# A second matrix product as seven block products for eight, with streamed weights and a transposed result, in an attention and feed-forward kernel

## The chip, the cores and the metric

The kernel runs on one core of a Trainium2 chip. A core has a matrix engine (TensorE, PE in the profile), a vector engine (VectorE, DVE), a scalar engine (ScalarE, ACT), a general engine (GpSimd, POOL) and a queue that issues transfers (SyncE, SP). They run side by side and wait for one another by semaphores. The metric is the device time of one execution in microseconds (us), lower is better. For a program on one core, runs agree to some tenths of a per cent; all runs quoted here count as fast ones. Before the change the time was 1672.99 us (median of 3 runs, 1670.59 to 1674.83).

## The reference

```python
# q, k, v: (8, 12, 448, 64); w_in: (768, 2048); w_out: (2048, 768)
q_n, k_n = rmsnorm(q, g_q), rmsnorm(k, g_k)
scores = np.matmul(q_n, k_n.transpose(0, 1, 3, 2)) / np.sqrt(64)
attn = softmax(scores)
x = np.matmul(attn, v).transpose(0, 2, 1, 3).reshape(3584, 768)
h = x @ w_in                       # first product
g = np.maximum(h, 0.0) ** 2
out = g @ w_out                    # second product
```

The weights arrive as 64-bit floats and are turned into 32-bit floats inside the kernel ("rounding" below), chunk by chunk, with integer and float instructions on VectorE, ScalarE and GpSimd.

## The kernel before

The work goes in four spans of two batches. A "unit" is a pair of heads of one batch; there are 12 units in a span. The first attention has nothing beside it but the rounding of `w_in`. Then come, three times, a first product of a span and an attention of the next span with the second product laid between its matmuls; then the last first product and the last second product, alone.

The first product already uses seven block products for eight: the operands are cut into 2 x 2 blocks, sums of blocks are multiplied, and sums of the seven results give the four result blocks. The weight blocks and their sums are made once, written to device memory (`w1s`) and streamed back for each span. The second product is a plain one, from weights that stay in SBUF, the working memory on the chip:

```python
def second_product(work, span):
    for t in range(0, 2 * S, P):                       # 7 blocks of 128 tokens
        osb = work.tile([P, DM], F32, tag="osb", name="osb")
        for half in range(2):
            cols = slice(half * HALF, (half + 1) * HALF)
            po = ps_m.tile([P, HALF], F32, tag="m", name="po")
            for f in chunks:                           # 16
                nc.tensor.matmul(po, gT[:, f, t:t + P], w2[:, f, cols], ...)
                ...                                    # after the last: copy to osb, osb to memory
                yield                                  # after each matmul
```

The end of a unit of attention. `pavs` is the sum of values and `tots` the sum of the exponents; each has one buffer in PSUM (the memory that the matmuls write to), which the next unit needs:

```python
def finish(work, i):
    rec = work.tile([P, S], F32, tag="rec", name="rec", bufs=1)
    nc.vector.reciprocal(rec, tots.pop(i))
    nc.vector.tensor_tensor(xT[...], pavs.pop(i)..., rec..., ALU.mult)
    ...
```

In the first attention the exponents are summed by TensorE (`pe_sums`, a product with ones). In the later ones GpSimd and VectorE add the four blocks of exponents, and TensorE has only one product with ones, to save TensorE time.

## Time and profile before

| stage | us | TensorE busy, us | GpSimd busy, us |
|---|---|---|---|
| attention of span 0, rounding of `w_in` | 192.2 | 145.0 | 144.1 |
| first product of span 0, rounding of `w_out` | 150.5 | 136.2 | 69.8 |
| attention of span 1 beside second product of span 0 | 257.9 | 249.2 | 115.7 |
| first product of a later span | 127 to 129 | all | 29 to 34 |
| last second product, to the end | 150.4 | 144.5 | 1.0 |

The table is read from the windows view, whose rows give the busy time of each engine in a stretch. Where TensorE is busy for the whole of a stretch, only less TensorE work makes it shorter. Where it is not, one must ask what it waits for. The prediction shows the lines; one more piece is VectorE at the end of a unit of the first attention whose end no rounding disturbs (timeline view; start, duration, engine, line, operation, output and inputs):

```profile
103.22 2.96 DVE L585 RECIPROCAL rec<-tot 128x448 f32<-128x448 f32 x1 [6.91 <-PE tot L577]
106.09 1.16 DVE L517 TENSOR_REDUCE rstd<-qkn 112x16 f32<-112x1024 f32 x1
107.17 0.94 DVE L586 TENSOR_TENSOR xT<-pav,rec 128x448 f32<-128x448 f32 x1
```

The next unit's first values matmul starts at 108.20 us, after the multiply. Between the reciprocal and the multiply stands a reduction of another unit's normalisation.

### The profile page before, as it was taken

To read this page: it belongs to the slowest core of one execution; us is meant where nothing else is said; L and a number is where in the kernel's file an instruction comes from. 1 tells how busy PE (TensorE), PEld (TensorE's weight loads), DVE (VectorE), ACT (ScalarE), POOL (GpSimd) and SP (SyncE) were. 2 spreads that over 40 slices of the span, in tenths; PEclk is the share of its full clock that TensorE was granted. 3 is DMA by queue.
4 is the path that set the end of the run, shared out by engine and by line. 5 is a ranking of instruction groups with operands and counts; after the bars stand their busy time and mean duration, and the time that the engine had idled before them with its cause. 6 is when DMAs were issued, how large, how long until landed. Compare 5 with 4: busy or idle time off the path is not lost.

```text
span 1667.2 us, 14210 instructions
## 1 busy us (share of the span) xinstructions
PE 1556.5 (93%) x5392; PEld 771.7 (46%) x5392; DVE 550.1 (33%) x548; ACT 452.5 (27%) x621; POOL 659.1 (40%) x482
## 2 busy tenths in 40 slices
PE   5768788899999999999999999999999999999998
PEld 2223244444444455554444445554444445555554
DVE  4676589323333332122333331122333341111000
ACT  4566346232222301122222211123222221110000
POOL 5787645345455412235444421224554521221000
PEclk9989999999999999999999999999999999999999
DMA  3655445321111113331111102331111102330000
GB/s 118 204 188 185 176 164 194 101 84 43 43 43 43 43 39 86 89 102 46 43 43 44 43 20 82 89 85 48 43 43 54 41 20 61 86 89 21 19 19 21
DMA packets 93393, 125.29 MB, mean 75 GB/s; under 512 B 7300, under 2 KB 87684, under 8 KB 93316
## 3 DMA queue, kind: packets, MB, share of 16 engines
q1 hardware_dynamic: 93316, 124.29, 24.3%
q8 instruction: 45, 0.74, 0.2%
q14 instruction: 32, 0.26, 0.0%
HBM read 102.24 MB, written 22.02 MB: 75 GB/s over the span
## 4 chain that ended last, share of the span: by engine, by line
PE 84%; DVE 4%; POOL 3%; issue 3%; ACT 3%; DMA 2%; SPq 0%; DVEq 0%; POOLq 0%; ACTq 0%
PE po L690 36%; PE sc L545 8%; PE pav L566 8%; PE pd L636 8%; PE pc L636 8%; PE pa L636 7%; PE pb L636 4%; PE tot L577 3%; PE pt L534 2%; ACT qkT L536 1%; DMA w1s<-gT 1%; POOL gT L450 1%; DVE gT L400 1%; POOL rstd L519 1%; DVE gT L401 1%
## 5 line engine op out<-in xcount | busy, mean ns | idle before, releaser
L690 PE MATMUL po<-w,gT 128*128 128x384 f32 x1792 | 597.4, 490 | 0.0
L690 PEld LDWEIGHTS po<-w,gT 128*128 128x128 f32 x1792 | 334.5, 190 | 269.1 <-issue 51.0
L641 POOL TENSOR_TENSOR gT<-gT 128x448 f32<-128x448 f32 x128 | 123.6, 968 | 384.8 <-ACT gT L640 384.8
L585 DVE RECIPROCAL rec<-tot 128x448 f32<-128x448 f32 x48 | 141.9, 2956 | 279.8 <-PE tot L577 279.8
L548 ACT ACTIVATE pr<-sc 112x896 f32<-112x896 f32 x192 | 166.1, 914 | 215.5 <-PE sc L545 215.4
L566 PE MATMUL pav<-pr,vt 112*64 112x448 f32 x768 | 177.2, 572 | 38.5 <-issue 38.5
L545 PE MATMUL sc<-qkT 64*112 64x448 f32 x768 | 172.2, 568 | 0.7 <-ACT qkT L536 0.7
L518 POOL TENSOR_SCALAR rstd<-rstd 112x16 f32<-112x16 f32 x48 | 37.6, 784 | 321.4 <-DVE rstd L517 320.5
L636 PE MATMUL pa<-xT,sw 128*128 128x448 f32 x384 | 156.8, 545 | 3.1 <-DVE rec L585 3.1
L519 POOL TENSOR_TENSOR rstd<-rstd,mhalf 112x16 f32<-112x16 f32 x48 | 142.5, 2968 | 4.0
L640 ACT ACTIVATE gT<-gT 128x448 f32<-128x448 f32 x96 | 55.2, 575 | 302.8 <-DVE gT L665 183.2
L536 ACT ACTIVATE qkT<-pt,gains 128x448 f32<-128x448 f32 x96 | 59.4, 632 | 276.2 <-PE pt L534 276.2
L517 DVE TENSOR_REDUCE rstd<-qkn 112x16 f32<-112x1024 f32 x48 | 58.2, 1212 | 186.3 <-ACT qkn L514 186.0
L566 PEld LDWEIGHTS pav<-pr,vt 112*64 112x64 f32 x768 | 49.8, 141 | 149.7 <-issue 147.0
L636 PEld LDWEIGHTS pa<-xT,sw 128*128 128x128 f32 x384 | 74.0, 193 | 76.0 <-issue 71.2
L521 POOL TENSOR_TENSOR qkn<-qk,rstd 112x512 f32<-112x512 f32 x96 | 100.8, 1071 | 3.8
L534 PE MATMUL pt<-ident,qkn 112*128 112x112 f32 x384 | 55.1, 271 | 45.6 <-ACT qkT L536 24.2
L545 PEld LDWEIGHTS sc<-qkT 64*112 64x112 f32 x768 | 61.7, 175 | 76.7 <-issue 64.7
L636 PE MATMUL pd<-xT,sw 128*128 128x448 f32 x192 | 80.1, 554 | 9.7 <-DVE z L656 9.7
L556 POOL TENSOR_TENSOR acc<-acc,pr 112x896 f32<-112x896 f32 x36 | 75.0, 2084 | 33.7 <-DVE acc L556 33.7
L554 POOL TENSOR_TENSOR acc<-pr 112x896 f32<-112x896 f32 x36 | 74.9, 2081 | 28.7 <-ACT pr L548 28.7
L696 ACT COPY osb<-po 128x384 f32<-128x384 f32 x28 | 13.4, 479 | 264.1 <-PE po L690 264.1
(61 smaller groups left out, 1294.7 us busy)
## 6 DMA issues: line engine op xcount, KB each, us to landing
sw<-w1s SPq DMA_DIRECT2D x224, 192.0 KB, 2.4
gT<-in_moe_w_in_dram SPq DMA_DIRECT2D x16, 768.0 KB, 6.6
gT<-in_moe_w_out_dram SPq DMA_DIRECT2D x16, 768.0 KB, 4.3
qk<-in_q_dram SPq DMA_DIRECT2D x48, 224.0 KB, 3.4
qk<-in_k_dram SPq DMA_DIRECT2D x48, 224.0 KB, 3.6
vt<-in_v_dram SPq DMA_DIRECT2D x48, 224.0 KB, 2.8
w1s<-gT SPq DMA_DIRECT2D x8, 1344.0 KB, 7.5
out_dram<-osb SPq DMA_DIRECT2D x28, 384.0 KB, 2.7
```

What stands on the lines that cost most here:

```text
L519: nc.gpsimd.tensor_tensor(rflat, rflat, mhalf, ALU.pow)
L521: nc.gpsimd.tensor_tensor(qkn[:, s].rearrange("p j h d -> p h j d"), qk[:, s].rearrange("p h (j d) -> p h j d", d=D), rstd[:, s].rearrange ...
L534: nc.tensor.transpose(pt[:, j * SP:(j + 1) * SP], qkn[:, s, j].rearrange("p h d -> p (h d)"), ident[:SP, :SP])
L536: nc.scalar.activation(qkT[:, s], pt, AF.Copy, scale=gains[:, s:s + 1])
L545: nc.tensor.matmul(sc[:, h, 0:S], qkT[rows, 1, c * SP:(c + 1) * SP], qkT[rows, 0, :], start=True, stop=True)
L548: nc.scalar.activation(pr, sc[:, :, 0:S], AF.Exp)
L556: (nc.vector if c == 2 else nc.gpsimd).tensor_tensor(accs[i], accs[i], pr, ALU.add)
L566: nc.tensor.matmul(pavs[i][h * D:(h + 1) * D, :], vs[i][:, h, c, :], pr[:, h, :], start=(c == 0), stop=(c == NJ - 1))
L585: nc.vector.reciprocal(rec, tots.pop(i))
L636: nc.tensor.matmul(ps, stream[n][:, c], rhs[:, c], start=first and c == 0, stop=c == HC - 1, skip_group_check=not first)
L641: nc.gpsimd.tensor_tensor(g, g, g, ALU.mult)
L690: nc.tensor.matmul(po, gT[:, f, t:t + P], w2[:, f, cols], start=(f == chunks[0]), stop=(f == chunks[-1]))
```

## The change

The second product, too, is to take seven block products for eight. That needs sums of the blocks of `w_out` (made once, written to memory as `w2s`, streamed back), sums of the blocks of its input (`combine`), and more room, so `w2` no longer stays in SBUF. The result now comes out transposed; TensorE transposes it back on the way out. Twice as many chunks now go through the costlier rounding with block sums, in 35 steps. They are spread: 10 in the first attention (19 before), 14 in the first product of span 0, and 11 in the first ten half units of the second attention (a unit is issued in two halves), which for that reason run without the second product. Units are normalised two ahead, not one, and the tokens stay in another order, so that the multiply in `finish` writes in order.

```diff
-    w2 = consts.tile([P, NFC, DM], F32, name="w2")
 ...
+    gC = consts.tile([P, 3, HF, S], F32, name="gC")
 ...
+    w2s = dram.tile([HC, 7, HF // 4, P, 4 * P], F32, name="w2s")
 ...
-        qkn = loads.tile([SP, 2, NJ, 2, D], F32, tag="qkn", name="qkn", bufs=1)
+        qkn = loads.tile([SP, 2, NJ, 2, D], F32, tag="qkn", name="qkn", bufs=2)
 ...
-        nc.vector.tensor_tensor(xT[:, t, hp, :].rearrange("d (p j) -> d j p", j=NJ),
-                                pavs.pop(i).rearrange("d (j p) -> d j p", j=NJ),
-                                rec.rearrange("d (j p) -> d j p", j=NJ), ALU.mult)
+        nc.vector.tensor_tensor(xT[:, t, hp], pavs.pop(i), rec, ALU.mult)
 ...
-            if i + 1 < end:
-                norm(i + 1)
+            if i + 2 < end:
+                norm(i + 2)
 ...
+    def combine(f):
 ...
+        sub(gC[:, 0, f], g12, g11, ALU.subtract)
+        sub(gC[:, 1, f], g22, gC[:, 0, f], ALU.subtract)
+        sub(gC[:, 2, f], g21, gC[:, 1, f], ALU.subtract)
+        sub(g12, g22, g12, ALU.subtract)
 ...
+        for m in range(HC):                        # in second_product
+            for i in uses2:                        # the seven block products
+                ps = ps_m.tile([P, S], F32, tag="m", name="ps")
+                for c in range(HF):
+                    load_blocks(n + 5)
+                    nc.tensor.matmul(ps, stream[n][:, c % 4], rhs_of[i][:, c], start=c == 0, stop=c == HF - 1)
 ...
+        def deliver(ct, col, t):
+            pt = ps_m.tile([P, 512], F32, tag="m", name="po")
+            for j in range(NJ):
+                nc.tensor.transpose(pt[0:SP, j * P:(j + 1) * P], ct[:, j * SP:(j + 1) * SP], ident)
+            osb = work.tile([SP, NJ, P], F32, tag="osb", name="osb")
+            nc.scalar.copy(osb.rearrange("p j n -> p (j n)"), pt[0:SP])
 ...
+    EARLY, ALONE = 10, 10
+    LATE = 2 * NFC + 3 - 11
 ...
+                    if u < alone:
+                        weights(LATE + 11 * (u + 1) // alone)
+                    elif u == alone and span == 0:
+                        for f in range(HF):
+                            combine(f)
```

## The prediction

> **What bounds the kernel now.** I read the page's busy line first, then a table by windows cut at the stage borders, then the chain that ended last, then the timeline of TensorE in the first stage, then the groups of GpSimd work.
>
> ```profile
> PE 1556.5 (93%) x5392; PEld 771.7 (46%) x5392; DVE 550.1 (33%) x548; ACT 452.5 (27%) x621; POOL 659.1 (40%) x482
> ...
> PE   5768788899999999999999999999999999999998
> ...
> POOL 5787645345455412235444421224554521221000
> ```
>
> TensorE is the bound from the ninth slice on. Before that it is not, and there GpSimd and VectorE are the fullest. The windows say how much. Columns: stretch, its length, then busy us and instruction count of PE, PEld, DVE, ACT, POOL, then granted clock, DMA share, GB/s.
>
> ```profile
> 18.35:208.00 189.65, 145.01 (x664) 56.89 (x664) 121.73 (x108) 107.78 (x132) 144.09 (x112) 0.90 0.53 172
> 210.50:300.00 89.50, 75.61 (x187) 36.12 (x188) 77.32 (x85) 48.83 (x65) 47.28 (x31) 0.96 0.54 183
> 300.00:361.00 61.00, 60.55 (x160) 30.51 (x162) 14.81 (x23) 14.37 (x24) 22.54 (x21) 0.95 0.29 81
> 361.00:619.00 258.00, 249.31 (x969) 123.10 (x966) 83.82 (x67) 68.02 (x89) 115.66 (x69) 1.00 0.14 42
> 619.00:747.00 128.00, 127.55 (x346) 64.51 (x346) 25.70 (x41) 24.25 (x43) 34.09 (x35) 1.00 0.32 90
> ...
> 1516.80:1667.20 150.40, 144.52 (x449) 84.81 (x447) 4.52 (x8) 3.93 (x8) 1.00 (x2) 0.99 0.05 19
> ```
>
> These are, in order: attention of the first pair of batches with the rounding of all of w1; the first part of the first product with the rounding of w2; its rest; attention of the next batches laid between the second product; a first product without weight work; and the last second product, alone. The two middle stages come three times. The first two rows hold about 45 and 14 us in which TensorE is idle, and a clock below 1; everything after is TensorE work end to end.
>
> ```profile
> 618.87 2.25 PE pa L636 x6
> 621.12 2.25 PE pb L636 x6
> 623.37 2.25 PE pc L636 x6
> ...
> 1516.84 144.49 PE po L690 x448
> ```
>
> The chain gives the true pace (busy means overlap): six instructions, three matmuls of 448 columns, in 2.255 us (step from 621.12 to 623.37 and on to 625.63), so 0.752 us a matmul; 448 instructions, 224 matmuls of 384 columns, in 144.49 us, so 0.645 us. Both are 1.68 ns a column: there is no fixed cost per matmul to win.
>
> **What the Trainium skill says.** "TensorE: Matmul & The Clock Gate", section "Part 1: The HAM clock gate", says that an idle stretch of about 3.4 us or more drops the clock to half, and takes as long to end. The trace agrees: after the 5.18 us pause below, four instructions span 1.76 us that span 0.97 us after a pause of 2.43 us.
>
> ```profile
> 108.20 0.97 PE L566 MATMUL pav<-pr,vt 112*64 112x448 f32 x4 [2.43 <-issue]
> ...
> 116.21 0.98 PE L534 MATMUL pt<-ident,qkn 112*128 112x112 f32 x8
> 117.13 1.76 PE L545 MATMUL sc<-qkT 64*112 64x448 f32 x8
> ...
> 124.07 1.76 PE L566 MATMUL pav<-pr,vt 112*64 112x448 f32 x4 [5.18 <-issue]
> ```
>
> "SBUF — State Buffer", section "SBUF: two separate sides", says that GpSimd and some VectorE operations lock each other out of a shared port pair. The trace fits: the same rounding multiply of 128x384 on GpSimd ran four in 4.07 us at 99.5 us and four in 5.22 us at 116.8 us, and its mean is 1323 ns. "PSUM — Partial Sum Buffer", section "Summary: rules for kernel authors", says that transfer to memory must go by way of an engine and SBUF; so the transposed result costs a PSUM copy as well as the transpose.
>
> **The change, part by part.**
>
> *Second product.* Removed: 224 matmuls of 384 columns a span, 144.5 us. Added: 3 x 7 x 8 = 168 of 448 columns, 168 x 0.752 = 126.3 us. That is 18.2 us a span. Also added: 12 output tiles of four transposes. Eight transposes of the same kind take 117.13 - 116.21 = 0.92 us above, so four take about 0.5; 12 x 0.5 = 6 us. Each is followed by a product whose PSUM buffer is being emptied (two buffers, and the transpose has taken the other): a VectorE add of this form takes 0.62 us, with some 0.3 us of pipeline and signalling, less the 0.5 us of transposes, so about 0.4 us of wait, 12 x 0.4 = 5 us. Net 126.3 + 11 = 137.5 us for 144.5: a gain of **7 us a span, 28 us in four**. This is all on TensorE, in stages that it bounds. The four extra subtractions per f (0.62 us each) and the seven adds per block row are on VectorE, which has 84 busy of 258 us there, so free. The streamed weights, 42 blocks of 256 KB in some 250 us, are well under the 90 GB/s that the first product already streams.
>
> *First stage.* 19 rounding steps become 10, and the normalisation is taken one unit earlier. The 12 units now take 189.65 us, 15.8 each. A unit that no rounding disturbs takes 13.1 us (transposes at 103.10 and 116.21), of which TensorE has 10.7 and waits 2.43 for the division at the end of a unit. In that wait VectorE does the reciprocal of 2.96 us, a reduction of the next normalisation of 1.16 us and the multiply of 0.94 us. With the reduction earlier and the multiply writing in order (0.62, as for other operations of its size) the unit should come to 11.8 us. So 12 x 11.8 = 142, plus 4 us of start, plus half of the 25 us by which the disturbed units exceed 13.1, less a little: 10 us. Sum 156 for 189.65: a gain of **34 us**.
>
> *First product of the first span.* It took 150.5 us against the undisturbed 128: 22 us lost to 16 chunks of w2. Now 14 steps lie in it, wider apart but heavier: each has two multiplies (2 x 1.32 us) and half of four additions of 1.0 us, 4.7 us of GpSimd for 2.0. I take 20 us of loss: a gain of 2 us.
>
> *The new stretch.* Ten of the 24 half units of the second attention now run with eleven rounding steps and no second product, because w2 is not ready before. TensorE has 5 x 8.5 = 42 us of work there (258 - 144.5 is 113 us for 12 units, 9.4 with waits). GpSimd has 5 normalisations (0.8 + 2.97 + 2 x 1.07 = 5.9 us) = 30, ten sums of 2.08 = 21, and ten chunks x 4.7 = 47: together 97 us, or about 87 where no lock stretches them. VectorE has 72 us. So **GpSimd becomes the bound** here. Then the last weights must be written to memory (the same write of w1 takes 7.5 us to land) and read back (2.4 us) before the first matmul. I take 105 us from the end of the first product to the first second-product matmul. After it: 137.5 us of second product and 6.5 units at 9.4, 61 us. Sum 303.5 for 258: a loss of **45 us**.
>
> Sum: -34 - 2 + 45 - 7 - 7 (two more joint stages) - 6 (the last, which ends with a copy and a transfer behind the transposes) = -11 us, from 1673 to some 1660.
>
> **The rivals.**
> First, the new stretch hides well: GpSimd is in step with a TensorE that paces each unit at some 12 us, and the stretch lasts 65 to 70 us. Against it: the 97 us of summed durations. If so the time is about 1625, faster.
> Second, the rounding moved into the first product stalls it: a load of w1 waits on GpSimd at the head of the one DMA queue, the weight stream waits behind it and behind 1344 KB writes of 7.5 us, while the stream is now only four blocks, 9 us, ahead. The stretch would need 56 x 192 + 14 x 768 + 7 x 1344 KB, some 31 MB, in 130 us: 240 GB/s, above the 212 GB/s of the busiest 50 us seen (100 to 150 us). For it: that arithmetic; against: no TensorE wait on such a load shows in the list of waits. It would add 20 to 30 us: 1685.
> Third, the deliveries cost more than 0.9 us each, for example by TensorE waiting for both PSUM buffers whenever attention's own transposes want one. At 1.5 us each the whole gain of the second product is gone: 1690.
> Fourth, the first stage stays disturbed, with stalls over 3.4 us that also halve the clock: 15 us back, 1675.
>
> **Range and chances.** The two large terms, -34 and +45, come from the same engine's queue and have errors of some 10 and 15 us; the second product's 28 us has an error of 8, the first product's of 10. Together about 22 us, so eight times in ten 1660 - 35 to 1660 + 35. The border of faster by 2% is 1639.5, about one such error away; the author's choice of ten and ten suggests a stretch fitted to the work, which speaks for the first rival. Chances: faster 0.2, same 0.76, slower 0.04.
>
> **What would show it.** Right: the last second product at 137 us from its first to its last matmul, with 0.7 to 1.1 us between blocks at each delivery; attention of the first stage ending near 174 us; GpSimd 85% busy or more and TensorE about 40% busy in the stretch after the first product, 95 to 115 us long; later joint stages of 250 us. Wrong: a last product above 144 us would break the first step; a stretch under 80 us breaks the claim that GpSimd bounds it, and then the kernel is faster by over 2%; a first product over 165 us would mean that its stream waited.

## The result, and the profile after

The changed kernel takes 1680.94 us (median of 4 runs, 1677.65 to 1683.29), the kernel before 1673.91 in the same rounds. The ratio is 1.0042, with a 95% interval of 1.0017 to 1.0067: a little slower, and within 2%. Ratios here and below are the mean time of one kernel's fast runs over that of the other's of the same rounds, so they are not quite the ratios of the medians.

First the busy line and the slices of the changed kernel:

```profile
PE 1524.6 (91%) x5136; PEld 711.4 (42%) x5136; DVE 643.9 (38%) x732; ACT 472.4 (28%) x653; POOL 705.2 (42%) x530
...
PE   4887899964599999999999999999999999999998
...
POOL 6665367799742430224555450224555420221000
```

TensorE is busy for 32 us less in sum, as a saving of block products should have it, but the span grew from 1667.2 to 1679.0 us. There is a new hole in the TensorE row, the ninth to eleventh slices, where GpSimd is full. The windows at the stage borders say how wide it is (columns as in the prediction):

```profile
18.28:196.80 178.52, 142.49 (x664) 55.83 (x664) 98.94 (x84) 90.11 (x112) 113.06 (x91) 0.90 0.36 111
196.80:333.10 136.30, 132.65 (x345) 66.36 (x345) 72.79 (x96) 57.11 (x82) 90.28 (x82) 0.97 0.70 231
333.10:452.47 119.37, 60.28 (x230) 22.39 (x229) 76.80 (x69) 53.36 (x65) 112.84 (x72) 0.71 0.49 154
452.47:655.18 202.71, 194.79 (x677) 90.80 (x678) 72.07 (x82) 42.95 (x58) 64.12 (x38) 0.99 0.29 84
...
783.00:1032.10 249.10, 238.53 (x905) 106.68 (x906) 91.50 (x85) 72.68 (x96) 115.54 (x69) 1.00 0.29 84
...
1535.30:1679.00 143.70, 134.41 (x385) 68.49 (x383) 15.72 (x26) 9.09 (x16) 0.96 (x2) 0.99 0.32 90
```

The third row is the new stretch of attention with rounding and no second product; the fourth, "the joint rest" below, is what is left of that attention, with the second product. In the stretch TensorE works for half of the time, at a mean clock of 0.71 (60.3 us, for 42 predicted at full clock), and GpSimd is busy for 112.8 of 119.4 us. Set side by side:

| stage | before, us | after, us | difference |
|---|---|---|---|
| first attention | 192.2 | 178.5 | -13.7 |
| first product of span 0 | 150.5 | 136.3 | -14.2 |
| second attention and second product of span 0 | 257.9 | 119.4 + 202.7 = 322.1 | +64.2 |
| the same of spans 1 and 2 | 257.7 and 256.0 | 249.1 and 248.0 | -8.6 and -8.0 |
| last second product, to the end | 150.4 | 143.7 | -6.7 |

The three later first products differ by half a us or less each. The rows sum to +13.0, with these to +11.8, the difference of the spans.

The gain of the second product is there. In its last pass, alone on TensorE (timeline view, three products and two deliveries):

```profile
1619.00 6.28 PE L715 MATMUL ps<-gT,sw 128*128 128x448 f32 x16 [0.28 <-DVE ct L729]
1625.12 0.60 PE L705 MATMUL po<-ident,ct 128*112 128x128 f32 x4
1625.99 6.28 PE L715 MATMUL ps<-gT,sw 128*128 128x448 f32 x16 [0.28 <-DVE ct L729]
1632.11 0.60 PE L705 MATMUL po<-ident,ct 128*112 128x128 f32 x4
1632.90 6.28 PE L715 MATMUL ps<-gT,sw 128*128 128x448 f32 x16 [0.19 <-ACT p L721]
```

A delivery costs 1625.99 - 1625.12 = 0.87 us, transposes and the wait for the buffer together. Eight matmuls take 6.1 us.

In the new stretch, this is what TensorE waits for (timeline, the last three units):

```profile
403.14 1.76 PE L578 MATMUL tot<-acc,ones 112*64 112x448 f32 x4 [13.43 <-POOL acc L557]
...
427.50 1.76 PE L578 MATMUL tot<-acc,ones 112*64 112x448 f32 x4 [12.35 <-POOL acc L557]
...
450.55 1.76 PE L578 MATMUL tot<-acc,ones 112*64 112x448 f32 x4 [11.03 <-POOL acc L557]
```

It waits for the softmax sums, which stand in GpSimd's queue behind rounding work. And GpSimd's own instructions are slow there. At one place in it, GpSimd and VectorE side by side (timeline):

```profile
411.52 6.83 POOL L457 TENSOR_TENSOR gC<-gC 128x384 f32<-128x384 f32 x1
...
412.31 0.55 DVE L435 TENSOR_SCALAR gC<-gC 128x768 uint32<-128x768 uint32 x1
412.79 0.61 DVE L632 TENSOR_TENSOR gC<-gT 128x448 f32<-128x448 f32 x1
...
417.52 1.64 DVE L443 SCALAR_TENSOR_TENSOR gC<-gC 128x768 f32<-128x768 uint32 x1
```

The same addition took 0.99 us in the first stage (at 113.61 us). Here its record spans a run of ten VectorE instructions without a gap. In the whole stretch the 20 block sums took 36.4 us on GpSimd (groups of its instructions; count, busy us, mean ns of one, idle time before):

```profile
L457 POOL TENSOR_TENSOR gC<-gC 128x384 f32<-128x384 f32 x5 | 12.2, 2444 | 0.4
...
L456 POOL TENSOR_TENSOR gC<-gC 128x384 f32<-128x384 f32 x5 | 10.2, 2032 | 0.3
L459 POOL TENSOR_TENSOR gC<-gC 128x384 f32<-128x384 f32 x5 | 7.4, 1479 | 0.4
L458 POOL TENSOR_TENSOR gC<-gC 128x384 f32<-128x384 f32 x5 | 6.6, 1326 | 0.2
```

### The profile page after: what moved, and what is told of

Same layout as the page of the kernel before. It is cut to its first block, busy times and chain, and to the rows that moved or that the text cites. A ratio compares the mean times of both kernels' runs of the same rounds, so it can differ in the third digit from the quotient of the medians.

```text
span 1679.0 us, 14449 instructions
## 1 busy us (share of the span) xinstructions
PE 1524.6 (91%) x5136; PEld 711.4 (42%) x5136; DVE 643.9 (38%) x732; ACT 472.4 (28%) x653; POOL 705.2 (42%) x530
## 4 chain that ended last, share of the span: by engine, by line
PE 78%; POOL 8%; issue 4%; DMA 3%; DVE 3%; ACT 3%; SPq 1%; POOLq 0%; DVEq 0%; ACTq 0%
PE ps L715 31%; PE pav L567 8%; PE sc L546 8%; PE pa L646 7%; PE pd L646 7%; PE pc L646 7%; PE tot L578 4%; PE pb L646 4%; POOL gC L451 2%; PE pt L535 2%; POOL acc L557 1%; DMA gC<-in_moe_w_out_dram 1%; ACT qkT L537 1%; POOL gC L457 1%; DMA w2s<-gC 1%
## 5 line engine op out<-in xcount | busy, mean ns | idle before, releaser
L715 PE MATMUL ps<-gT,sw 128*128 128x448 f32 x768 | 307.7, 549 | 7.3 <-DVE ct L729 3.6
L715 PE MATMUL ps<-gC,sw 128*128 128x448 f32 x576 | 229.4, 545 | 3.7 <-ACT osb L707 2.0
L715 PEld LDWEIGHTS ps<-gT,sw 128*128 128x128 f32 x768 | 141.9, 191 | 158.6 <-issue 141.1
L546 PE MATMUL sc<-qkT 64*112 64x448 f32 x768 | 176.1, 577 | 4.4 <-ACT pr L549 3.7
L715 PEld LDWEIGHTS ps<-gC,sw 128*128 128x128 f32 x576 | 106.6, 190 | 116.4 <-issue 108.4
L519 POOL TENSOR_SCALAR rstd<-rstd 112x16 f32<-112x16 f32 x48 | 30.6, 637 | 252.4 <-DVE rstd L518 251.4
L707 ACT COPY osb<-po 112x512 f32<-112x512 f32 x48 | 28.1, 585 | 267.5 <-PE po L705 262.2
## 6 DMA issues: line engine op xcount, KB each, us to landing
sw<-w2s SPq DMA_DIRECT2D x168, 256.0 KB, 2.8
```

What stands on the lines that cost most here:

```text
L546: nc.tensor.matmul(sc[:, h, 0:S], qkT[rows, 1, c * SP:(c + 1) * SP], qkT[rows, 0, :], start=True, stop=True)
L715: nc.tensor.matmul(ps, stream[n][:, c % 4], rhs_of[i][:, c], start=c == 0, stop=c == HF - 1)
```

## The experiments

All ran on the chip beside the kernel before. Times are medians; all results were correct except where said.

**1. Softmax sums of the stretch on TensorE.** The edit:

```diff
+            pe = pe_sums or i < first + pe_units     # pe_units: 5 in span 1
-            scores(work, i, 0, pe_sums)
+            scores(work, i, 0, pe)
 ... (the same for the other uses of pe_sums)
```

> The changed kernel, with the softmax sums of the five units that run without the second product done by TensorE (matmuls with ones), as in the first stage, not by additions on GpSimd and VectorE. Theory: GpSimd's queue bounds that stretch (112.8 of 119.4 us busy there; the ten sums on GpSimd are 22.7 us of it). The stretch should shrink by nearly that, from 119 to 96-102 us, and the time from 1681 to some 1660 us, although TensorE gets 30 more matmuls. Rival: the sums are only where TensorE's wait shows, and the true bound is the chain of one unit after another (scores, exponent, values, division, at a halved clock); then another wait takes the place, the stretch stays at 114 us or more and the time at 1675-1683.

Measured: 1666.97 us against 1670.95, ratio 0.9963 (0.9937 to 0.9988). The stretch took 107.8 us (334.7 to 442.5), with GpSimd busy for 85.9. So it fell by 11.6 us, half of the 22.7 us of sums taken off GpSimd. The edit also takes VectorE's five additions (9.6 us) out of the stretch, and the 20 block sums on GpSimd now took 24.8 us for 36.4. Both expectations missed: GpSimd's load counts, but as it falls another wait appears. TensorE now waits for `pav`, the buffer of the values (timeline, the third and fourth unit):

```profile
385.18 1.76 PE L567 MATMUL pav<-pr,vt 112*64 112x448 f32 x4 [12.54 <-issue]
...
407.55 1.76 PE L567 MATMUL pav<-pr,vt 112*64 112x448 f32 x4 [10.15 <-issue]
```

The VectorE rows before 385 us show why (timeline of VectorE):

```profile
376.25 1.72 DVE L435 TENSOR_SCALAR gC<-gC 128x768 uint32<-128x768 uint32 x1 [4.84 <-DMA w2s<-gC]
377.89 2.94 DVE L586 RECIPROCAL rec<-tot 128x448 f32<-128x448 f32 x1
383.61 0.93 DVE L435 TENSOR_SCALAR gC<-gC 128x768 uint32<-128x768 uint32 x1 [2.77 <-DMA gC<-in_moe_w_out_dram]
384.46 0.61 DVE L587 TENSOR_TENSOR xT<-pav,rec 128x448 f32<-128x448 f32 x1
```

A rounding instruction stood at the head of its queue for 4.84 us until the writing of the last blocks to memory had ended, the reciprocal came behind it, and behind that another rounding instruction that waited 2.77 us for a load, before the multiply that frees the buffer.

**2. No rounding of w_out at all (wrong result).** The edit skips the steps, keeps loads and writes, and writes stale blocks:

```diff
+        if n >= NFC and step < 3:
+            if step == 2:
+                load_w(n + SETS)
+            return
```

> Wrong result on purpose: the changed kernel, with none of the rounding and combining work for w2; the blocks written to memory are stale ones. Loads, writes and everything else stay. It measures what making w2's blocks costs. Theory (GpSimd bounds the stretch): without it the stretch takes attention's own pace, five units of some 12.5 us plus a few us for write and read, 65-75 us for 119; the first product of the first span loses its last stalls (136 to about 131). Time about 1625. Rival (the stretch is bound by the chain through the engines at a halved clock): the stretch stays at 100 us or more and the time above 1655.

Measured: 1633.41 us, ratio 0.9776 (0.9750 to 0.9802; whether over or under 2% is unclear); the result was wrong. First product 130.9 us, stretch 78.8 us (323.1 to 401.9). So the arithmetic on `w_out` costs 119.4 - 78.8 = 40.6 us of the stretch, and the rival falls. The stretch came out 4 us, and the time 8 us, longer than the theory had it. Its transfers stay, and the mean busy share of the DMA engines rose from 0.49 to 0.80.

**3. Three steps moved from the stretch to the first product.**

```diff
-    EARLY, ALONE = 10, 10
-    LATE = 2 * NFC + 3 - 11
+    EARLY, ALONE = 10, 8
+    LATE = 2 * NFC + 3 - 8
-                        weights(LATE + 11 * (u + 1) // alone)
+                        weights(LATE + 8 * (u + 1) // alone)
```

> The changed kernel with three rounding steps moved from the stretch into the first product of the first span (17 there for 14, 8 in the stretch for 11, and 8 half units alone for 10). Theory: the first product lost only 8 us to 14 steps (136 for 128), so three more cost it 2 to 6 us, and the stretch ends 25-32 us sooner, of which the two half units that now go beside the second product take some 9 back: time 1655-1668. Rival (the prediction's second: the weight stream of the first product is at its limit, 231 GB/s now): the first product grows by 15 us or more, and the time is 1672 or more.

Measured: 1671.89 us, ratio 0.9999 (0.9967 to 1.0032). The first product took 140.7 us (195.7 to 336.4, 4.4 more), the stretch 96.6 (22.8 less), the joint rest 211.9 (9.2 more). The first product takes a step for 1.5 us; the weight stream does not stall it, so the second rival of the prediction falls. The total missed the expectation by 4 us (1655 to 1668), since the stretch saved less than 25 us. By the ratios (0.9999 for 1.0042) it is some 7 us less than that of the changed kernel.

**4. Early release of the values in the first stage.**

```diff
+        src = pavs.pop(i)
+        if b < 2:
+            nc.scalar.copy(xT[:, t, hp], src)
+            src = xT[:, t, hp]
         nc.vector.reciprocal(rec, tots.pop(i))
-        nc.vector.tensor_tensor(xT[:, t, hp], pavs.pop(i), rec, ALU.mult)
+        nc.vector.tensor_tensor(xT[:, t, hp], src, rec, ALU.mult)
```

> The changed kernel; in the first stage only, ScalarE copies a unit's sum of values out of PSUM at once, and the division works on the copy. The next unit's first matmul then waits for a copy of 0.53 us, not for reciprocal, reduction and multiply (2.94, 1.22 and 0.61 us). Theory: this wait of 2.10 us in each undisturbed unit (and up to 5.6 in disturbed ones, with half a clock after it) is what kept the first stage at 14.9 us a unit for the 11.8 predicted, and the reduction that still sits in it is the step that failed. Units should fall from 12.8 to about 10.7-11.3, the stage from 178.5 to 150-158 us, the time to 1655-1661. Rival (exponents or GpSimd's rounding hold the units, and the wait would go elsewhere): the stage stays above 170 us.

Measured: 1657.15 us against 1670.95, ratio 0.9907 (0.9885 to 0.9930). The first stage took 155.9 us (18.2 to 174.1) for 178.5: the theory holds. An undisturbed unit by its transposes, in the changed kernel and then now (timelines):

```profile
65.81 0.98 PE L535 MATMUL pt<-ident,qkn 112*128 112x112 f32 x8
...
78.60 0.98 PE L535 MATMUL pt<-ident,qkn 112*128 112x112 f32 x8
```

```profile
82.37 0.99 PE L535 MATMUL pt<-ident,qkn 112*128 112x112 f32 x8
...
92.98 0.98 PE L535 MATMUL pt<-ident,qkn 112*128 112x112 f32 x8
```

That is 92.98 - 82.37 = 10.6 us, TensorE work alone, where the changed kernel had 78.60 - 65.81 = 12.8. The disturbed units still take 15.2 to 16.6 us.

**5. Control: the same early release in the kernel before.** The edit is that of experiment 4, with the reordering write kept.

> Control: the kernel before, with the early release alone (ScalarE copies a unit's values out of PSUM in the first stage). If the wait for the division was a fault of the first stage in both kernels, the kernel before gains nearly as much from it as the changed one did (23 us): time 1648-1656. Rival (in the kernel before, rounding fills GpSimd and VectorE for 144 and 124 of 192 us, so the wait only moves to them): gain of 10 us or less, time above 1660. Either way this is the fair kernel to compare the mended change with.

Measured: 1669.55 us against 1670.51, ratio 0.9986 (0.9967 to 1.0005): the same. The rival was right. The first stage took 192.3 us (18.2 to 210.5), and TensorE waits elsewhere in it (timeline):

```profile
85.83 2.01 PE L534 MATMUL pt<-ident,qkn 112*128 112x112 f32 x8 [3.48 <-POOL qkn L521]
...
119.65 2.01 PE L534 MATMUL pt<-ident,qkn 112*128 112x112 f32 x8 [3.47 <-POOL qkn L521]
```

It waits for the normalisation on GpSimd, which is busy for 164.4 us of the stage with 19 rounding steps (144.1 before, with the same 112 instructions; why they took longer no run shows). So the early release alone is not enough: the 23 us of experiment 4 need something of the change as well. Fewer rounding steps in the stage and normalising earlier are the likely parts, but no run separates them. Without the early release the changed kernel could not collect the 23 us.

**6. Early release in the first stage and the stretch, with the sums on TensorE.** Experiments 1 and 4 together, the copy for `i < 2 * NPAIR + 5`.

> The changed kernel with the early release in the first stage and in the five units of the stretch, and the softmax sums of those five units on TensorE. When the sums alone went to TensorE, GpSimd fell to 85.9 of 107.8 us and TensorE's waits moved to the values of the next unit (12.5 and 10.2 us): they waited for the division on VectorE, in whose queue a rounding instruction stood in front that waited for the writing of the last blocks to memory. Theory: the copy frees the values' buffer from this, and the stretch shrinks from 107.8 to 95-101 us; first stage 156 us; time 1638-1644. Rival: the wait goes over to the sums' buffer, which is still freed by the reciprocal behind the same rounding instruction: stretch stays at 105-108, time 1644-1650.

Measured: 1636.57 us, ratio 0.9795 (0.9774 to 0.9815). First stage 154.7 us (18.2 to 172.9), stretch 102.4 us (307.6 to 410.0). The time came out 1.4 us under the theory's range; the stretch stayed 1.4 us above it, and below the rival's. Whether this version is faster than the kernel before by 2% is unclear.

**7 and 8. The same with 8 and with 6 steps in the stretch.** As experiment 3, with 4 and 3 units summed on TensorE.

> As early_and_sums, with three rounding steps moved from the stretch to the first product (17 and 8; 8 half units alone, 4 units with sums on TensorE). eight_steps alone was worth some 9 us on the changed kernel: first product 4.4 us longer, stretch 22.8 us shorter, the joint rest 9.4 us longer. Theory: the same here, since it is GpSimd and VectorE work that moves: time 1630-1637. Rival: with the sums gone from GpSimd the stretch is no longer bound by that work, and moving it gains under 4 us: 1637-1643.

> As early_sums_eight with five steps moved (19 in the first product, 6 in the stretch, 6 half units alone, 3 units with sums on TensorE). If the first product still takes them at 1.5 us a step, it gains another 3-6 us: 1626-1634. If its engines or its weight stream are now full (it moved 231 GB/s with 14 steps), it stalls by more than the stretch saves: 1636 or more.

Measured: 1633.98 us (5 rounds, ratio 0.9769, 0.9753 to 0.9786) and 1632.32 us (0.9772, 0.9756 to 0.9788). With six steps the first product took 144.8 us (172.9 to 317.7) and the stretch 64.6, but the joint rest 222.5 (to 604.8), as it takes in four more half units. Both times lie in the range of the theory, and both are faster than the kernel before by over 2%. From eight to six steps nothing can be told apart. From eleven to eight the gain is 2.6 us by the medians and some 4 by the ratios (0.9769 for 0.9795), where the theory had some 9 and the rival under 4; the intervals overlap. Stretch and joint rest share the attention, so what the one loses in length the other mostly takes. TensorE ends the stretch of experiment 8 with a wait for the weights (timeline):

```profile
382.22 8.07 PE L720 MATMUL ps<-gT,sw 128*128 128x448 f32 x16 [5.41 <-DMA sw<-w2s]
```

**9. Block sums of w_out on VectorE.** Of the changed kernel, for the pairs made in the stretch:

```diff
+            eng = nc.gpsimd if n < 23 else nc.vector
-            nc.gpsimd.tensor_tensor(b[S1], b[A21], b[A22], ALU.add)
+            eng.tensor_tensor(b[S1], b[A21], b[A22], ALU.add)
 ... (and the three others)
```

> The changed kernel with the block sums of the last five pairs of w2 chunks (those made in the stretch) on VectorE, not on GpSimd. On GpSimd these 20 instructions took 36.4 us there (up to 6.83 us for one that takes 1.0 us in the first stage). Theory: GpSimd bounds the stretch, and the excess of its time over the 97 us predicted is locking by VectorE's two-input instructions; the stretch falls from 119 to 90-100 us, with VectorE at 88-92 us busy for 77, and the remaining GpSimd instructions keep means of 1.2 us (multiplies) and 2.2 us (sums): time 1655-1664. Rival: VectorE, which gets 11-20 us more, takes over as the bound, or locks GpSimd's other work for longer: stretch above 108 us, time 1670 or more.

Measured: 1674.03 us, ratio 0.9995 (0.9967 to 1.0024). Here the theory fell: some 8 us less than the changed kernel by the ratios, 26 to 17 were expected. GpSimd lost 26 us of its load, and the stretch still took 112.6 us (334.3 to 446.9), as the rival had it. The window of this kernel's stretch and the longest waits of TensorE in it (sum row of the windows view, then the timeline):

```profile
sum 112.59, PE 57.48 PEld 19.79 DVE 95.91 ACT 53.78 POOL 86.86; mean PE 57.48 PEld 19.79 DVE 95.91 ACT 53.78 POOL 86.86
```

```profile
423.64 3.25 PE L568 MATMUL pav<-pr,vt 112*64 112x448 f32 x8 [14.84 <-issue]
446.92 1.86 PE L716 MATMUL ps<-gT,sw 128*128 128x448 f32 x2 [14.98 <-DMA sw<-w2s]
```

VectorE is now the fullest, and TensorE waits for it (the multiply that frees `pav` ends at 423.54 us) and for the weights. GpSimd's remaining work did not become faster either: its two softmax sums a unit rose from means of 2.2 and 2.3 us to 2.6 and 2.9.

**10. The same in the best version so far** (experiment 8 with the last three pairs' sums on VectorE).

> As early_sums_six, with the block sums of the last three pairs of w2 chunks on VectorE. There the stretch is 64.5 us for 3 units, and TensorE ends it with a wait of 5.4 us for the weights to come back from memory. If GpSimd still sets when the last blocks are written, the stretch falls by 4-8 us and the time to 1624-1629; if VectorE's queue sets it by now (rounding, division), nothing is gained or some us are lost: 1631-1637.

Measured: 1628.06 us (1626.27 to 1631.14), ratio 0.9734 (0.9709 to 0.9759). The time is in the first range, but the stretch fell by only 1.4 us (64.6 to 63.1) and the profiled span by 2.6. Its interval overlaps that of experiment 8 in part, so whether the VectorE sums help is not settled. TensorE no longer waits for the weights at the end of the stretch (timeline):

```profile
380.69 6.28 PE L721 MATMUL ps<-gT,sw 128*128 128x448 f32 x16
```

Its longest wait there is now 8.28 us, for the reciprocal that frees the buffer of the sums. It is the fastest version run: 2.7% faster than the kernel before, some 2.5% faster than that kernel with the same early release (0.9986), and faster than the changed one.

## Why the prediction was right or wrong

The time lay in the predicted range and in the likeliest class, but the sign was wrong: the sum of the terms was -11 us, and +11.8 us of span came (+7 us in the medians). Of these 22.8 us, the first stage is 20.3 (-13.7 for -34), the stretch and the joint rest 19.2 (+64.2 for +45); the first product gave 12.2 back (-14.2 for -2), the rest 4.5. That the time stayed inside the range is in part luck: the miss of the first product paid for half of another. By its steps:

**The second product: right.** Predicted 137.5 us of TensorE a span: the last one ran from 1535.3 to 1672.6, 137 us, with 0.87 us a delivery for the 0.9 predicted (transposes 0.60 for 0.5, the wait 0.27 for 0.4). The later joint stages gained 8.6 and 8.0 us for 7, the last 6.7 for 6. The third rival, dearer deliveries, did not come.

**The first product of span 0: mis-sized, to the good.** The term "20 us of loss" measured 8 (136.3 for 128). The prediction reckoned that heavier steps would stall TensorE as much as the 16 chunks had. GpSimd had room for them (busy for 90 of 136 us), and experiment 3 shows 1.5 us for each added step.

**The first stage: mis-sized.** Predicted -34, measured -13.7. The step that failed is "With the reduction earlier and the multiply writing in order ... the unit should come to 11.8 us". The multiply did become shorter (0.61 us for 0.94), and no more: the reduction did not move. VectorE in an undisturbed unit of the changed kernel (timeline):

```profile
123.53 2.96 DVE L586 RECIPROCAL rec<-tot 128x448 f32<-128x448 f32 x1 [10.31 <-PE tot L578]
126.40 1.16 DVE L518 TENSOR_REDUCE rstd<-qkn 112x16 f32<-112x1024 f32 x1
127.48 0.61 DVE L587 TENSOR_TENSOR xT<-pav,rec 128x448 f32<-128x448 f32 x1
```

Normalising two units ahead changed which unit is reduced, not where the reduction stands in VectorE's order. So an undisturbed unit took 12.8 us, which would be 12 us more over twelve units than forecast, and the stage ended at 196.8 us, not near 174. The rest of the miss, some 10 us, is in the other units: three of 17.6 to 18.3 us, with pauses of 4.44 to 5.63 us, and two of 14.5 us. In those two the pause was the usual 2.10 us, and half the clock came after it all the same, as the first of these lines shows (timeline):

```profile
83.37 1.75 PE L567 MATMUL pav<-pr,vt 112*64 112x448 f32 x4 [2.10 <-issue]
...
97.85 0.97 PE L567 MATMUL pav<-pr,vt 112*64 112x448 f32 x4 [2.10 <-issue]
```

Of seven pauses of 2.10 us in the stage, three were followed by half pace and four by full pace. So the 3.4 us that the prediction cites fit the two pauses that it shows, but are no border on which a plan can rest here.

Experiment 4 took the wait away and the stage came to 155.9 us, which shows that the wait at the end of the units cost the 22 us. That this is the 156 of the prediction is luck: it came from undisturbed units of 10.6 us, not 11.8, and disturbed ones longer than forecast. Experiment 5 shows that it takes something of the change itself to get there.

**The new stretch: mis-sized.** Predicted 105 us to the first matmul of the second product, measured 119.4. The sum of GpSimd work failed by one term, the block sums: 20 instructions at 1.0 us were forecast and 36.4 us came, the others lay within some 2 us of their terms. The last block sum ended at 443.06 us, and the write and the read back took 9.4 us more, as forecast (7.5 + 2.4). I had the lock of the two engines among the citations and did not apply it to this term. The timeline suggests that VectorE holds GpSimd up there, and it fits what the Trainium skill says of the shared port pair ("SBUF — State Buffer", section "SBUF: two separate sides", cited in the prediction): while one of the two engines has the pair, the other waits. It is not shown, as no run took the lock alone away. Experiment 1 comes nearest: with additions gone from both queues the same block sums took 24.8 us.

**"GpSimd becomes the bound": half right.** Its queue was the fullest, and the first rival (the stretch hides well) did not come. But experiment 9 took 26 us off it and gained 7 us of stretch, and experiment 1 took 22.7 off and gained 11.6. VectorE, 76.8 us busy, also stands in order, and its rounding instructions wait for loads and for the writing of blocks. TensorE's next unit needs both queues in turn; that this is why the stretch stays long is argued from the waits, not isolated by a run. The stretch fell by 40.6 us when the work was taken away altogether (experiment 2), by 22.8 when three steps of it, and two half units, were moved out (experiment 3), and by another 5.4 after experiment 1 when the values' buffer no longer needed VectorE (experiment 6). In whole time, moving work out of the stretch (some 7 us) and moving it from GpSimd to VectorE (some 8 us) can't be told apart.

**The size of the loss** in the joint rest was forecast at 198.5 us and came to 202.7, a small miss. The wait of 5.4 us for the last blocks that ended the stretch in experiment 8 is gone in experiment 10, and the stretch is only 1.4 us shorter. What stays open is what sets its length there.

## What to carry to other kernels

Fewer TensorE operations are worth their time only where TensorE is the bound, and what prepares them has to run somewhere: here 23 us won in three later stages were lost, and more, in one stretch where the preparation had nothing to hide behind. When a sum of durations names the fullest engine, look at the second fullest and at what stands in each queue's order before trusting the sum: where one chain passes through two queues, taking load off one of them may only move the wait, as in experiments 1 and 9. Free a scarce buffer with the engine that is idle (one copy of 0.53 us, in place) rather than at the end of a chain of three instructions, and check in the trace what the next wait will be.

## What the Trainium skill lacked or had wrong

- "SBUF — State Buffer", section "Who interferes with whom", says that the loser of the shared port pair is blocked for the other's whole instruction. It does not say whether a run of VectorE instructions without gaps can hold one GpSimd instruction up throughout, as the trace suggests but no run isolates: an addition of 0.99 us has a record of 6.83 us beside ten VectorE instructions, another one of 5.47 us.
- "TensorE: Matmul & The Clock Gate", section "Part 4: PE-mode transpose", gives some 275 ns for a transpose of 128x128 in bf16 in a kernel. The median record of one in 32 bits is 259 ns here (112x112), but eight in a row start within 0.92 us (the first at 105.86, the next matmul at 106.78), so 0.115 us each is what they cost; the section has no such figure.
- "GPSIMD Engine Reference" has no figure for a power: raising 16 numbers in each of 112 partitions took 2.95 us, more than an addition of 896 (2.1 us).
